# Scaling a weight matrix late: the first batch multiplies by lambda at its output

## The chip, the cores and the metric

The kernel runs on one core of one Trainium2 chip. The metric is device time in microseconds (us), as the median of several executions. Before the change it is 306.67 us, the median of 5 runs that lie between 305.12 and 307.16 us. TensorE, the matrix engine, is called PE below, and its weight loads are PEld. VectorE is DVE, ScalarE is ACT, GpSimd is POOL and SyncE is SP.

## The reference

Block-sparse attention over 4 batches, 8 heads, 768 tokens and head size 64 is followed by a residual MLP with affine scalings. Attention keeps a mask of blocks of 32: neighbours, first and last blocks, and three sampled blocks for each row of blocks. Then:

```python
a1 = alpha1 * x + beta1
tok = np.einsum('ts,bsd->btd', w_tok, a1)
u = x + lam * tok
a2 = alpha2 * u + beta2
ch = np.maximum(a2 @ w_ch1, 0.0) @ w_ch2
return (u + lam * ch).astype(np.float32)
```

`x` is the attention output, batch x 768 x 512. `w_ch1` is 512 x 2048 and `w_ch2` is 2048 x 512. `lam` has one value for each of the 512 output columns, so `lam * (h @ w_ch2)` equals `h @ (w_ch2 * lam)`: lambda may be multiplied into the columns of the weights, or into the result.

## The kernel before

**The tiling.** The 32 heads of the 4 batches are taken as 16 pairs of heads. The scores of one pair are cut into 9 units of 128 x 1024. For each unit PE multiplies queries and keys (L924 for the first six pairs, L943 for the other ten), ACT takes the exponential (L962), DVE multiplies by the mask (L967, only for pairs 6 to 15), and PE multiplies with the values (L986). DVE divides by the row sums (L1002, L1005). Then comes the token mixing, PE's L1207 with DVE's L1158, L1169, L1231 and L1245 around it.

**The channel MLP** works on half batches, counted `kk` from 0 to 7; `kk` 0 and 1 are batch 0. Its first product (L1354) makes 16 tiles of 128 x 384, each of four matmuls. ACT (L1393) or DVE (L1401) adds a bias, takes the relu and writes it to `hts`, of which there are two buffers. The second product (L1434) makes three output tiles (`mt`) of 128 x 512, each from four groups (`r`) of four matmuls, group `r` reading rows `4r` to `4r+3` of the weight tile `w2b`. DVE adds the result to `x_sb` (L1456), and SP sends it out (L1475). Half batch `kk` can start its first product only when `hts` has a free buffer, that is, when the second product of `kk - 2` is through.

**The second weights** are loaded by POOL in four DMAs (L588) and then scaled in place by DVE: eight instructions (L678) multiply two rows of blocks each by a bf16 copy of lambda (`lam_bcb`, L670). Every group of the second product depends on the two of them that scaled its rows (L1447).

**The start.** The first pair of heads does not go through POOL. SP and ACT issue its loads at L360 to L366: `sampi` and both heads of k on ACT's queue, both heads of q and then three small constant loads (`ind_dr`, L366) on SP's queue. Each head is cast to bf16 (L421), transposed by PE (L426) and copied out of PSUM by four DVE copies (L455), two for q and two for k, after which the first score matmul can run.

**The order of the work** is written by a planner (`Plan`, L104 to L271). Every operation has dependencies, a cost on each engine that may take it, and a due time. The planner walks through time and gives each free engine the ready operation with the earliest due time. Each engine then executes exactly that order (`pin_order`, L56). The engines start the plan at fixed times (L465: PE, ACT at 6200 ns, DVE at 6250 ns), and the loads of the second head of the first pair are assumed to land at the times in L894. Before the planner runs, the due times are shifted by random numbers from a list of seeds (L489 to L494). A new list, or another way of drawing, gives another order of everything on every engine.

Of the kernel before, what the change touches and what calls it, by code (L numbers as in the profile page):

```python
# [3 lines left out]

# [16 lines left out]
ALU = mybir.AluOpType  # L21
# [4 lines left out]
D = 64  # L26
# [3 lines left out]
DM = 512  # L30
FF = 4 * DM
P = 128
NT = S // P
# [10 lines left out]
NXB = 3  # L44
# [1 line left out]
EXPB = -0.35667494  # L46
T0 = 6
FINE = 3
SEEDS = [3000002, 3000003, 3000005, 3000006, 3000008, 3000027, 3000041, 3000052, 3000078, 3000097, 3000108, 3000114, 3000122, 3000127, 3000136, 3000180, 3000188, 3000206, 3000215, 3000219, 3000250, 3000263, 3000275, 3000280, 3000283, 3000293, 3000304, 3000326, 3000332, 3000343, 3000367, 3000440, 3000558, 3000615, 3000616, 3000621, 3000657, 3000851, 3000855, 3000993, 3001011, 3001012, 3001029, 3001046, 3001124, 3001231, 3001486, 3001568, 3001676, 3001731, 3001993, 3002553, 3003152, 3003308, 3003443, 3004176, 3005076, 3005643, 3006518, 3007963, 3008413, 3008734, 3008895]
NFILL = 24  # L50
ORD = ((0, 2, 4, 1, 3, 5), (1, 3, 5, 0, 2, 4))
HF = 3 * S
# [24 lines left out]
def dve(n, rate=1):  # L77
    return n / 0.96 / rate + 155
# [196 lines left out]
def kernel(  # L275
# [17 lines left out]
    nc = tc.nc  # L293
# [5 lines left out]
    ind_dr = nc.inline_tensor(ind_np, name="ind_c")  # L299
# [14 lines left out]
    kx2 = [t[:, 1, :, :] for t in qk2]  # L314
    qkr = [t[0:D].rearrange("p w h (g r t) -> p w h g r t", g=3, r=2) for t in qk2]
# [4 lines left out]
    x_sb = pp.tile([P, NXB * NT, DM], FP, name="x_sb", tag="x_sb")  # L320
    lam_bc = pp.tile([P, DM], FP, name="lam_bc", tag="lam_bc")
# [4 lines left out]
    lam_bcb = pp.tile([P, DM], BF, name="lam_bcb", tag="lam_bcb")  # L326
# [20 lines left out]
    ot = many(2, [P, DM], FP, "ot")  # L347
    rcp = many(2, [P, NT], FP, "rcp")
    MB = slice(D, KC)
# [4 lines left out]
    def pair_ap(src, b, n):  # L354
        return src[b, 2 * n : 2 * n + 2].rearrange("h (p o) d -> p h (o d)", o=NT)
# [4 lines left out]
    nc.scalar.dma_start(sampi[MB, :], sampled_blocks.bitcast(I32))  # L360
    nc.sync.dma_start(q2f[:, 0, :], pair_ap(q, 0, 0)[:, 0, :])
    nc.scalar.dma_start(k2f[:, 0, :], pair_ap(k, 0, 0)[:, 0, :])
    nc.scalar.dma_start(k2f[:, 1, :], pair_ap(k, 0, 0)[:, 1, :])
    nc.sync.dma_start(q2f[:, 1, :], pair_ap(q, 0, 0)[:, 1, :])
    for i in range(1, 4):
        nc.sync.dma_start(kx2[i // 2][MB, i % 2, :], ind_dr.ap())  # L366

# [29 lines left out]
    def where(out, what, op, lim):  # L399
# [9 lines left out]
        out=eqt[MB, :, 0:NR],  # L409
        in0=sampi[MB, 0 : 2 * NR : 2].unsqueeze(1).broadcast_to([NBLK, NBLK, NR]),  # L410
        in1=kbi[MB, :].unsqueeze(2).broadcast_to([NBLK, NBLK, NR]),
        op=ALU.is_equal,
    )
    nc.vector.tensor_reduce(
        out=mbb[MB, :], in_=eqt[MB], axis=mybir.AxisListType.X, op=ALU.max
# [14 lines left out]
    for w in (0, 1):  # L430
# [13 lines left out]
        out=qx2[0][MB, 0, 0:HS],  # L444
        in0=bq_ps[0][0:NBLK, 0:HS],
# [6 lines left out]
    for w in range(2):  # L452
        t = transposes(gbT[w][:], lambda o: relp[:, 0, w, ts(o, P)], range(3))
        for r in range(2):
            nc.vector.tensor_copy(  # L455
                out=qkr[0][:, w, 0, :, r, :], in_=t[r * D : (r + 1) * D, 0:3]
            )
    keep_warm(10, P)
    for t in vext:
        nc.vector.memset(t[:, :, :, D:VW], 1.0)  # L460
# [1 line left out]

    pl = Plan(
        dict(sps=2, gb=4, eT=NE, q=4, k=4, v=4, vx=3, qk=2, hts=2, a1p=2, ub=2, ot=2),
        dict(PE=6200, ACT=6200, DVE=6250, POOL=4000, SP=4000),  # L465
    )
    GB = [("gb", 0), ("sps", 0)]
    GL = [("gb", 0), ("sps", 0)]
# [1 line left out]
    def bank(key):  # L470
        p, j = pl.slot[key]
        return (gbT if p == "gb" else spsT)[j]

    def sl(key):
        return pl.slot[key][1]
# [64 lines left out]
    def landed(name, t):  # L540
        op = Op(name, [], 0, None)
        op.start, op.vis = 0, t
        return op
# [20 lines left out]
    W1, W2, BC = [], [], {}  # L564
    w2h = {}
# [66 lines left out]
    for g in range(4):  # L632
# [6 lines left out]
                deps=[x.tr for x in WTT],  # L639
# [9 lines left out]
        deps=[BC["a1"], BC["lam"]],  # L649
# [6 lines left out]
        deps=[BC["b1"], BC["lam"]],  # L656
# [6 lines left out]
        deps=[landed(("be2",), 6500)],  # L663
    )
    B1T = []
    LB = pl.dve(
        ("lamb",),
        dve(512, 2),
        46,
        lambda op: nc.vector.tensor_copy(out=lam_bcb[:], in_=lam_bc[:]),  # L670
        deps=[BC["lam"]],
    )
    W2S = []
    for g in range(8):

        def e_w2(op, g=g):
            w = w2h["t"][:, 2 * g : 2 * g + 2, :]
            nc.vector.tensor_tensor(  # L678
                out=w, in0=w, in1=lam_bcb[:].unsqueeze(1).broadcast_to([P, 2, DM]), op=ALU.mult
            )  # L680

        W2S.append(pl.dve(("w2s", g), dve(1024, 2), 52 + g, e_w2, deps=[W2[g // 2], LB]))


    last = None
# [202 lines left out]
    for i in range(2):  # L888
        op = pl.dve(
            ("fc", i),  # L890
            dve(384, 2),
            1 + 0.1 * i,
            lambda op, i=i: first_cast(1, i, nc.vector.tensor_copy),
            deps=[landed(("f", i), 5000 + 1350 * i)],  # L894
        )
        FC1.append(op)
    ROWS = []
# [10 lines left out]
    NORM = {}  # L908
    OT = {}
    CH1S = {}  # L910
    UTD = {}

    def unit_heads(u):
# [100 lines left out]
    for pi in range(NP):  # L1014
        b, n = divmod(pi, NPAIR)
# [7 lines left out]
        def e_v(op, pi=pi):  # L1023
# [10 lines left out]
            deps=[LD[("v", pi)]],  # L1034
# [6 lines left out]
    i = 0  # L1041
    while i < NI:
# [5 lines left out]
        deps = []  # L1048
# [14 lines left out]
        if pi == 0:  # L1063
            deps = [] if u < 4 else deps + ROWS[:1]
        if pi == 1:
            deps = deps + ROWS[1 : 2 if u < 4 else 3]
        occ = 437 if pi < T0 else 850
        op = pl.pe(
            ("qk", i),
            occ,  # L1070
            i - 0.7,
            e_qk,
            deps=deps,
            after=prevq[-1:],
            need=[(key, [("sps" if len(ks) == 1 else "gb", 0)]) for ks in keys for key in ks],
            uses=uses,
# [3 lines left out]
        for j, key in zip(batch, keys):  # L1080
# [6 lines left out]
                deps=[op],  # L1087
# [6 lines left out]
            if units[j][0] >= T0:  # L1094
# [5 lines left out]
                    deps=[ex] + MASK,  # L1100
# [3 lines left out]
            for a in unit_heads(uj):  # L1104
# [8 lines left out]
                    lambda op, part, pj=pj, uj=uj, a=a: emit_pv(op, part, pj, uj, a),  # L1113
# [10 lines left out]
    for pi in range(NP):  # L1124
# [211 lines left out]
        for hf in range(2):  # L1336
# [89 lines left out]
            for mt, c0, c1 in cuts:  # L1426
                t = 3 * hf + mt
                cs = slice(c0, c1)
                ck = ("cp", kk, mt, c0)
                for r in range(4):  # L1430

                    def e_c2(op, hk=hk, ck=ck, mt=mt, r=r, cs=cs):
                        for nk in range(4 * r, 4 * r + 4):
                            nc.tensor.matmul(  # L1434
                                bank(ck)[:, cs],
                                htsT[hk][:, nk, ts(mt, P)],
                                w2h["t"][:, nk, cs],
                                start=(nk == 0),
                                stop=(nk == 15),
                            )  # L1440

                    c2 = pl.pe(
                        ("ch2", kk, mt, r),
                        pe(4, 4 * (c1 - c0)),
                        d0 + 18 + (4 * mt + r) * 18 / 12 + c0 / 100,
                        e_c2,
                        deps=rel[4 * r : 4 * r + 4] + W2S[2 * r : 2 * r + 2],  # L1447
                        after=pc[-1:],
                        need=[(ck, GL)] if r == 0 else [],
                        uses=[hk] + ([] if r == 0 else [ck]),  # L1450
                    )
                    pc.append(c2)
                okey = ("ot", kk, mt, c0)

                def e_ot(op, okey=okey, ck=ck, b=b, t=t, cs=cs):
                    nc.vector.tensor_tensor(  # L1456
                        out=ot[sl(okey)][:, cs],
                        in0=x_sb[:, b % NXB * NT + t, cs],
                        in1=bank(ck)[:, cs],
                        op=ALU.add,  # L1460
                    )

                o = pl.dve(
                    ("ot", kk, mt),
                    dve(c1 - c0),
                    d0 + 18 + 18 / 12 * 4 * mt - 2,
                    e_ot,
                    deps=[c2],
                    need=[(okey, [("ot", 0)])],
                    uses=[ck],  # L1470
                )
                OT[(b, t)] = o

                def e_out(op, okey=okey, b=b, t=t, cs=cs):
                    nc.sync.dma_start(  # L1475
                        out[b].rearrange("(p o) d -> p o d", o=NT)[:, t, cs],
                        ot[sl(okey)][:, cs],
                    )

                pl.add(  # L1480
                    ("out", kk, mt),
                    [("SP", 450, beside(350, 450, 90))],
                    0,
                    e_out,
                    deps=[o],
                    uses=[okey],
                )

    for seed in SEEDS:
        r = random.Random(seed)  # L1490
        part, step = r.choice([0.01, 0.03, 0.1, 0.3]), r.choice([0.5, 1.5, 4])
        for op, due in zip(pl.ops, [op.due for op in pl.ops]):
            if r.random() < part and op.due0 < 300:
                op.due = due + r.gauss(0, step)
    pl.run()
    pin_order(nc, tc)

# [29 lines left out]
```

## Time and profile before

| | |
|---|---|
| median of 5 runs | 306.67 us |
| the profiled execution, its own time | 307.16 us |
| its span, first to last instruction | 305.4 us |
| granted PE clock | 1.000 |
| PE busy | 299.7 us |
| DVE busy | 229.0 us |
| ACT busy | 179.8 us |
| POOL busy | 44.8 us |

The profile comes from one execution. Its own time is 0.49 us above the median of the runs, and 1.76 us of it lie outside the span. PE's busy time counts overlapping matmuls once, but it also counts the time that a matmul needs to fill and drain. A PE that is 98% busy is therefore not proof that it streams data 98% of the time. A matmul of 512 columns is shown with some 380 ns, yet a run of them starts one every 216 ns. Where it matters the text works with these distances from start to start.

### The profile page before, as it was taken

The numbers are of one execution on the slowest core, as the hardware profiler recorded it, in microseconds if no ns is written. First come the engines' busy times: TensorE is split into PE (matmuls) and PEld (weight loads), VectorE is DVE, ScalarE is ACT, GpSimd is POOL, SyncE is SP. The second block draws the span as 40 slices with busy tenths as digits, with TensorE's granted clock in tenths as the row PEclk, the third lists the DMA queues.
The fourth block names the chain that finished last, engine by engine and source line by source line (L and its number), as shares of the span: only waits on it lengthen the run. The fifth ranks groups of instructions, "written<-read, shape, count | busy, mean of one in ns | idle before, by whom it ended". The sixth has DMA issues, their size and how long they took to land.

```text
span 305.4 us, 7168 instructions
## 1 busy us (share of the span) xinstructions
PE 299.7 (98%) x2970; PEld 188.4 (62%) x2996; DVE 229.0 (75%) x434; ACT 179.8 (59%) x246; POOL 44.8 (15%) x71
## 2 busy tenths in 40 slices
PE   8998999999999999999999999999999999999997
PEld 4776877766655575556654675555755574555545
DVE  7669999998888786978685797867986863837622
ACT  3998889897697847887467835768756410000000
POOL 9365344323002000120000000000000000000000
PEclk9999999999999999999999999999999999999999
DMA  7999999999669628763160406132002004000012
GB/s 161 194 240 199 206 203 206 200 154 178 108 119 114 137 28 146 144 115 63 55 146 13 102 36 120 46 80 68 2 24 64 34 8 136 16 34 34 36 65 73
DMA packets 50672, 31.38 MB, mean 103 GB/s; under 512 B 27784, under 2 KB 47056, under 8 KB 50640
## 3 DMA queue, kind: packets, MB, share of 16 engines
q0 software_dynamic: 17520, 15.47, 34.3%
q1 hardware_dynamic: 32796, 15.06, 21.2%
q8 instruction: 23, 0.38, 0.5%
q10 hardware_dynamic: 324, 0.39, 0.4%
q14 instruction: 9, 0.07, 0.1%
HBM read 30.78 MB, written 6.29 MB: 121 GB/s over the span
## 4 chain that ended last, share of the span: by engine, by line
PE 87%; DMA 7%; POOL 2%; ACT 2%; issue 1%; DVE 1%; POOLq 0%; ACTq 0%
PE gb L1434 27%; PE gb L1354 27%; PE gb L1207 10%; PE gb L986 10%; PE sps L943 4%; PE sps L924 4%; DMA wtk<-in_moe_w_tok_dram 3%; DMA q<-in_q_dram 3%; PE gb L943 3%; ACT eT L962 2%; PE gb L426 1%; DVE eT L967 1%; POOL k L552 0%; POOL wtokT L379 0%; POOL wtk L574 0%
## 5 line engine op out<-in xcount | busy, mean ns | idle before, releaser
L962 ACT ACTIVATE eT<-sps 128x1024 f16<-128x1024 f32 x114 | 111.0, 1032 | 8.2 <-PE sps L924 7.3
L1354 PE MATMUL gb<-uT,w1b 128*128 128x384 bf16 (+1 forms) x512 | 93.7, 326 | 0.0
L1434 PE MATMUL gb<-w2b,hts 128*128 128x512 bf16 (+2 forms) x374 | 88.5, 370 | 1.4 <-issue 0.2
L1354 PEld LDWEIGHTS <-w1b 128*128 128x128 bf16 x512 | 47.7, 98 | 33.7 <-issue 3.2
L967 DVE TENSOR_TENSOR eT<-eT,msk 128x1024 f16<-128x1024 f16 x90 | 59.3, 685 | 5.4 <-ACT eT L962 5.4
L986 PEld LDWEIGHTS <-eT 128*128 128x128 f16 x1152 | 48.6, 97 | 18.1 <-issue 3.4
L1434 PEld LDWEIGHTS <-hts 128*128 128x128 bf16 x400 | 36.4, 98 | 37.0 <-issue 1.9
L986 PE MATMUL gb<-vext,eT 128*128 128x65 f16 x1152 | 54.0, 193 | 0.5 <-ACT eT L962 0.2
L1393 ACT ACTIVATE hts<-gb,b1t 128x384 bf16<-128x384 f32 x64 | 36.8, 584 | 27.3 <-PE gb L1354 24.2
L962 ACT ACTIVATE eT<-gb 128x512 f16<-128x512 f32 x60 | 32.5, 595 | 32.7 <-PE gb L943 32.6
L1401 DVE TENSOR_SCALAR hts<-gb,b1t 128x384 bf16<-128x384 f32 x64 | 39.3, 616 | 15.4 <-PE gb L1354 14.4
L1456 DVE TENSOR_TENSOR ot<-x_sb,gb 128x512 f32<-128x512 f32 (+2 forms) x25 | 16.6, 664 | 26.4 <-PE gb L1434 26.3
L1207 PE MATMUL gb<-a1p,wtokT 128*128 128x256 bf16 (+1 forms) x360 | 34.6, 251 | 0.0
L924 PE MATMUL sps<-qk 88*128 88x512 bf16 (+1 forms) x144 | 32.8, 333 | 0.6 <-ACT eT L962 0.2
L1207 PEld LDWEIGHTS <-wtokT 128*128 128x128 bf16 x360 | 29.2, 98 | 4.0
L1231 DVE TENSOR_TENSOR x_sb<-x_sb,gb 128x512 f32<-128x512 f32 (+1 forms) x26 | 16.7, 645 | 6.9 <-PE gb L1207 6.7
L1005 DVE TENSOR_TENSOR x_sb<-gb,rcp 128x384 f32<-128x384 f32 x32 | 17.8, 557 | 1.1
L943 PE MATMUL sps<-qk 64*128 64x256 bf16 x180 | 17.9, 305 | 0.0
L943 PEld LDWEIGHTS <-qk 64*128 64x128 bf16 x240 | 9.2, 94 | 11.5 <-issue 6.6
L552 POOL DMA_DIRECT2D q<-in_q_dram x15 | 10.7, 711 | 38.0 <-DMA qk<-q 33.6
L1245 DVE TENSOR_TENSOR ub<-x_sb,a_bc 128x512 bf16<-128x512 f32 (+1 forms) x26 | 15.9, 644 | 0.1
L1158 DVE TENSOR_TENSOR a1p<-x_sb,a_bc 128x768 bf16<-128x768 f32 (+1 forms) x17 | 15.4, 906 | 0.2
(67 smaller groups left out, 163.7 us busy)
## 6 DMA issues: line engine op xcount, KB each, us to landing
out_dram<-ot SPq DMA_DIRECT2D x23, 256.0 KB, 2.2
v<-in_v_dram POOLq DMA_DIRECT2D x16, 192.0 KB, 9.6
k<-in_k_dram POOLq DMA_DIRECT2D x15, 192.0 KB, 8.4
q<-in_q_dram POOLq DMA_DIRECT2D x15, 192.0 KB, 9.5
w1b<-in_moe_w_ch_dram POOLq DMA_DIRECT2D x4, 512.0 KB, 12.4
w2b<-in_moe_w_ch_dram POOLq DMA_DIRECT2D x4, 512.0 KB, 11.5
qk<-qk SPq DMA_DIRECT2D x20, 96.0 KB, 2.9
wtk<-in_moe_w_tok_dram POOLq DMA_DIRECT2D x3, 384.0 KB, 9.2
```

Of the source, the lines that this page charges most:

```text
L924: nc.tensor.matmul(spsT[sl(key[0])][:, o : o + w], kx2[i][0:KC, a, ts(jt, P)], qx2[i][0:KC, a, c : c + w], start=True, stop=True,)
L943: nc.tensor.matmul(half(key, r)[:, o : o + w], kd[i][rows, h, g, :], qx2[i][rows, h, c : c + w], start=True, stop=True,)
L962: nc.scalar.activation(out_, in_, AF.Exp, bias=EXPB, scale=SCALE)
L967: nc.vector.tensor_tensor(out=e, in0=e, in1=msk[:, :, x : x + 512], op=ALU.mult)
L986: nc.tensor.matmul(bk[:, t * VW : t * VW + D + 1], eTt[sl(("eT", i))][:, ts(col, P)], vx[:, a, jt, 0 : D + 1], start=(r == 0), stop=(r >= ...
L1005: nc.vector.tensor_tensor(out=x_sb[:, s0 : s0 + NT, h * D : (h + 1) * D], in0=o[:, :, 0:D], in1=rc[:].unsqueeze(2).broadcast_to([P, NT, D] ...
L1207: nc.tensor.matmul(bank(bk)[:, j * wp * P : (j + 1) * wp * P], wtokT[:, s, ts(m * g + j, P)], a1p[sl(ak)][:, s, 0:wp, :].rearrange("p w c ...
L1231: nc.vector.tensor_tensor(out=s, in0=s, in1=tp, op=ALU.add)
L1354: nc.tensor.matmul(bank(bk)[:, 0 : HS + w0], w1b[:, dk, ts(f, P)], rhs[dk], start=(dk == 0), stop=(dk == 3),)
L1393: nc.scalar.activation(htsT[hk][:, f, :], bank(bk)[:, w0 : HS + w0], AF.Relu, bias=b1t[:, f : f + 1], scale=1.0,)
L1401: nc.vector.tensor_scalar(out=htsT[hk][:, f, :], in0=bank(bk)[:, w0 : HS + w0], scalar1=b1t[:, f : f + 1], scalar2=0.0, op0=ALU.add, op1=A ...
L1434: nc.tensor.matmul(bank(ck)[:, cs], htsT[hk][:, nk, ts(mt, P)], w2h["t"][:, nk, cs], start=(nk == 0), stop=(nk == 15),)
```

## The change

Four things are edited.

1. **Second weights.** The eight scaling instructions are no longer issued when the weights have landed. The first batch (`kk` 0 and 1) multiplies by unscaled weights, and its second product depends on the load of its rows only. Its output takes two DVE instructions in place of one: PSUM times `lam_bc` into `ot`, then `x_sb` plus `ot` into `ot`. The scaling instructions are added to the plan behind the second product of `kk` 1, with due times 96 to 99.5 in place of 52 to 59. The two for the rows of group `r` depend on all six products of the first batch that read these rows; from `kk` 2 on, group `r` depends on the two of them, as before.
2. **The start.** The three constant loads on SP's queue are issued between the two heads of q, and no longer behind them. The two copies of k out of PSUM move from DVE to ACT.
3. **The planner's constants.** The engines' start times and the assumed landing times of the second head change.
4. **The random shifts.** The list of seeds is another, and each seed now shifts only operations whose due time is near a random middle.

```diff
     nc.scalar.dma_start(k2f[:, 0, :], pair_ap(k, 0, 0)[:, 0, :])
+    for i in range(1, 4):
+        nc.sync.dma_start(kx2[i // 2][MB, i % 2, :], ind_dr.ap())
     nc.scalar.dma_start(k2f[:, 1, :], pair_ap(k, 0, 0)[:, 1, :])
     nc.sync.dma_start(q2f[:, 1, :], pair_ap(q, 0, 0)[:, 1, :])
-    for i in range(1, 4):
-        nc.sync.dma_start(kx2[i // 2][MB, i % 2, :], ind_dr.ap())
...
         for r in range(2):
-            nc.vector.tensor_copy(
-                out=qkr[0][:, w, 0, :, r, :], in_=t[r * D : (r + 1) * D, 0:3]
-            )
+            cp = nc.scalar.copy if w else nc.vector.tensor_copy
+            cp(out=qkr[0][:, w, 0, :, r, :], in_=t[r * D : (r + 1) * D, 0:3])
...
-        dict(PE=6200, ACT=6200, DVE=6250, POOL=4000, SP=4000),
+        dict(PE=5800, ACT=6050, DVE=5800, POOL=4000, SP=4000),
...
     W2S = []
-    for g in range(8):
-
-        def e_w2(op, g=g):
-            w = w2h["t"][:, 2 * g : 2 * g + 2, :]
-            nc.vector.tensor_tensor(
-                out=w, in0=w, in1=lam_bcb[:].unsqueeze(1).broadcast_to([P, 2, DM]), op=ALU.mult
-            )
-
-        W2S.append(pl.dve(("w2s", g), dve(1024, 2), 52 + g, e_w2, deps=[W2[g // 2], LB]))
+
+    def scale_w2(readers):
+        for g in range(8):
+
+            def e_w2(op, g=g):
+                w = w2h["t"][:, 2 * g : 2 * g + 2, :]
+                lam2 = lam_bcb[:].unsqueeze(1).broadcast_to([P, 2, DM])
+                nc.vector.tensor_tensor(out=w, in0=w, in1=lam2, op=ALU.mult)
+
+            W2S.append(
+                pl.dve(
+                    ("w2s", g),
+                    dve(1024, 2),
+                    96 + g / 2,
+                    e_w2,
+                    deps=readers[g // 2] + [LB],
+                )
+            )
...
-            deps=[landed(("f", i), 5000 + 1350 * i)],
+            deps=[landed(("f", i), 5600 - 500 * i)],
...
-                        deps=rel[4 * r : 4 * r + 4] + W2S[2 * r : 2 * r + 2],
+                        deps=rel[4 * r : 4 * r + 4] + (W2S[2 * r : 2 * r + 2] if kk > 1 else [W2[r]]),
...
+                    if kk < 2:
+                        RD.setdefault(r, []).append(c2)
...
-                    nc.vector.tensor_tensor(
-                        out=ot[sl(okey)][:, cs],
-                        in0=x_sb[:, b % NXB * NT + t, cs],
-                        in1=bank(ck)[:, cs],
-                        op=ALU.add,
-                    )
+                    o = ot[sl(okey)][:, cs]
+                    x = x_sb[:, b % NXB * NT + t, cs]
+                    ps_ = bank(ck)[:, cs]
+                    if b == 0:
+                        nc.vector.tensor_tensor(out=o, in0=ps_, in1=lam_bc[:, cs], op=ALU.mult)
+                        nc.vector.tensor_tensor(out=o, in0=x, in1=o, op=ALU.add)
+                    else:
+                        nc.vector.tensor_tensor(out=o, in0=x, in1=ps_, op=ALU.add)
...
-                    dve(c1 - c0),
+                    dve(c1 - c0) * (2 if b == 0 else 1),
...
+                if kk == 1 and mt == 2:
+                    scale_w2(RD)
...
-        part, step = r.choice([0.01, 0.03, 0.1, 0.3]), r.choice([0.5, 1.5, 4])
-        for op, due in zip(pl.ops, [op.due for op in pl.ops]):
-            if r.random() < part and op.due0 < 300:
-                op.due = due + r.gauss(0, step)
+        part, step = r.choice([0.02, 0.1, 0.3, 1]), r.choice([0.3, 1, 3])
+        mid, wide = r.uniform(0, 300), r.choice([4, 12, 40])
+        for op in pl.ops:
+            if abs(op.due0 - mid) < wide and r.random() < part:
+                op.due += r.gauss(0, step)
```

The two lists of seeds (63 numbers before, 52 after) are left out.

More of the change, by code (lines that the diff above doesn't have):

```diff
@@ L1 @@
-import random
 import random
@@ L48 @@
 FINE = 3
-SEEDS = [3000002, 3000003, 3000005, 3000006, 3000008, 3000027, 3000041, 3000052, 3000078, 3000097, 3000108, 3000114, 3000122, 3000127, 3000136, 3000180, 3000188, 3000206, 3000215, 3000219, 3000250, 3000263, 3000275, 3000280, 3000283, 3000293, 3000304, 3000326, 3000332, 3000343, 3000367, 3000440, 3000558, 3000615, 3000616, 3000621, 3000657, 3000851, 3000855, 3000993, 3001011, 3001012, 3001029, 3001046, 3001124, 3001231, 3001486, 3001568, 3001676, 3001731, 3001993, 3002553, 3003152, 3003308, 3003443, 3004176, 3005076, 3005643, 3006518, 3007963, 3008413, 3008734, 3008895]
+SEEDS = [2368360002, 2368360005, 2368360008, 2368360022, 2368360028, 2368360031, 2368360050, 2368360067, 2368360083, 2368360085, 2368360089, 2368360096, 2368360144, 2368360155, 2368360159, 2368360198, 2368360204, 2368360219, 2368360231, 2368360262, 2368360291, 2368360306, 2368360309, 2368360457, 2368360521, 2368360740, 2368360741, 2368360761, 2368360886, 2368360958, 2368361005, 2368361131, 2368361149, 2368361207, 2368361276, 2368361304, 2368361308, 2368361391, 2368361405, 2368361424, 2368361614, 1368351946, 1368351960, 1368352029, 1368352547, 1368352791, 1368352820, 2368362950, 2368362973, 2368363005, 2368363029, 1368353383]
 NFILL = 24
@@ L910 @@
     CH1S = {}
+    RD = {}
     UTD = {}
```

## The prediction

> **What bounds the kernel now.** First the page's shares and slices, to see which engine is full and where.
>
> ```profile
> PE 299.7 (98%) x2970; PEld 188.4 (62%) x2996; DVE 229.0 (75%) x434; ACT 179.8 (59%) x246; POOL 44.8 (15%) x71
> ...
> DVE  7669999998888786978685797867986863837622
> ACT  3998889897697847887467835768756410000000
> ```
>
> DVE is nearly full only in slices 4 to 10 (23 to 76 us); ACT is full up to about 70 us and has nothing left behind 245 us. PE is busy everywhere, so the question is how much of that is streaming. I took the start times of all matmuls in the trace and counted as lost whatever a distance from start to start exceeds the steady distance of its shape (0.216 us for 512 columns, 0.163 for 384, 0.109 for 256, 0.055 for 128, 0.030 for the value products). From 9 us to the end this gives 13.4 us lost: 0.72 in 10 to 20, 1.96 in 20 to 30, 0.08 in 30 to 40, 0.93 in 40 to 50, 0.54 in 50 to 60 (4.2 us in all) and 9.2 us behind 60, spread at 0.2 to 0.9 for each 10 us. The last is the drain around each L943 batch and each change of product; the change leaves these alone. So **PE is the bound**, and what an edit away from PE can win lies mostly ahead of 60 us. The waits and the timeline show the largest piece there:
>
> ```profile
> 26.72 0.40 PE L986 MATMUL gb<-vext,eT 128*128 128x65 f16 x8
> ...
> 27.86 0.34 PE L426 MATMUL gb<-identb,q 128*128 128x128 bf16 x3 [0.74 <-DMA q<-in_q_dram]
> ```
>
> PE stands 0.9 us here (26.93, the last value product, to 27.86) for a load of q. The chain of waits has this load too ("DMA wtk" from 6.25, then "DMA q" 18.09 to 27.8): ahead of 28 us the chain is POOL's queue of loads, and its first issues are not touched by the edit.
>
> Then the instructions that the change touches, by group and in time:
>
> ```profile
> L678 DVE TENSOR_TENSOR w2b<-w2b,lam_bcb 128x1024 bf16<-128x1024 bf16 x8 | 5.4, 681 | 0.0
> L648 DVE TENSOR_TENSOR a_bc<-a_bc,lam_bc 128x512 f32<-128x512 f32 x1 | 0.7, 678 | 0.0
> L1456 DVE TENSOR_TENSOR ot<-x_sb,gb 128x512 f32<-128x512 f32 x23 | 15.8, 685 | 24.2 <-PE gb L1434 24.1
> ```
>
> The eight scalings (51.3 to 69.5 us) are far ahead of their first use at 81.5 us.
>
> **Part 1, the start.** Rows:
>
> ```profile
> 1.20 0.41 SPq L364 DMA_DIRECT2D q2f<-in_q_dram  x1
> 1.40 0.36 ACTq L362 DMA_DIRECT2D k2f<-in_k_dram  x1
> 1.67 1.20 SPq L366 DMA_DIRECT2D qk<-ind_c  x3
> ...
> 4.29 0.51 ACT L421 CAST relp<-k2f 128x384 bf16<-128x384 f32 x1 [0.74 <-DMA k2f<-in_k_dram]
> 4.83 0.48 ACT L440 ACTIVATE qk<-gb 24x384 bf16<-24x384 f32 x1
> 4.92 1.50 DVE L455 COPY qk<-gb 64x384 bf16<-64x384 bf16 x4 [0.42 <-PE gb L426]
> ```
>
> ACT waits 0.74 us for the first head of k. In front of it on the wire are both heads of q. The second moves behind three issues of 0.40 us, from 1.20 to 2.40, and the three small loads (36 KB each, 108 KB) go ahead of it in place of its 192 KB. The 84 KB difference is 0.5 us at the 161 GB/s of the first slice; k lands earlier by 0 to 0.5, I take 0.3. The copies: DVE's four end at 6.42, and the first k copy, which the first score matmul needs, at about 6.05. On ACT the k copies come behind L440 (ends 5.31) at some 0.48 each (L440's row, the nearest PSUM source of 384 columns): 5.9 and 6.3. That is 0.1 better; with k earlier 0.4, so the first score matmul moves from 6.22 to about 5.8. The price: the second head of q lands 1.2 us later, by the median of 2.5 us at 4.9; its cast is at 7.65, so nothing. Everything up to 26.9 us could come 0.4 earlier (ACT is 9.9 of 10 us busy in 10 to 20). Then PE meets the load of q at 27.86, which hangs on POOL's queue, and waits longer. Between 0 and -0.4; nearest to the former, **-0.1**.
>
> **Part 2, scaling leaves 51 to 69 us.** DVE instructions without a wait between them start faster than their duration: three L967 of 0.685 take 1.89, one each 0.60 us. So eight of L678 take 8 x 0.605 = 4.84 us of DVE. DVE was 9.39 and 9.70 us busy in 50 to 60 and 60 to 70, PE lost 0.54 and 0.10 there. The gain is between 0 and 0.64, because PE can't win back more than it lost; the 0.93 of 40 to 50 lies ahead of the first scaling. DVE is the fullest engine there, so near the upper end: **-0.5**. The first product of batch 0 fills PE from 56 us on, so DVE's relief beyond that is earlier work, not time.
>
> Here a rule of the Trainium skill differs from the row: "VectorE: DVE Perf Modes", section "The DRAIN you can't avoid", says that a next instruction starts only when the pipeline has emptied (and points to a later section for exceptions). By it the scalings hold DVE for 8 x 0.681 = 5.45 us. The row decides: 4.84. The sum stays as it is, since PE's 0.64 caps the gain in both.
>
> **Part 3, two output instructions in the first batch.** Six outputs at 86.6 to 148.4 us. L1456's 0.685 for the PSUM product (same shape), then an addition in SBUF, row L648, 0.678, which reads what was just written. A dependent pair is L1158 and L1169: starts 104.92 and 105.92, 1.00 apart at a duration of 0.96, so 0.04 more. Added: 6 x 0.72 = 4.3 us of DVE in 62 us, where it idles 10 to 35% of each 10 us. "VectorE: DVE Perf Modes", "Rules for kernel authors", speaks against this: chained instructions gain nothing by being close, one should keep their number low. By the rule alone, all exposed, the sum is +4.3; by the row it is hidden in idle time of DVE, and the output DMA behind it has no reader. The bank comes free after the first of the two as before, though the planner reckons it with the second. From 0 to +4.3; **0**.
>
> **Part 4, scaling in place between batches 0 and 1.** In the trace the last second product of `kk` 1 ends at about 148.4 and the first of `kk` 2 is at 151.7.
>
> ```profile
> 144.00:149.00 5.00, 4.95 (x54) 3.32 (x53) 3.24 (x6) 0.30 (x2) 0.00 (x0) 1.00 0.00 0
> 149.00:154.00 5.00, 4.95 (x56) 3.52 (x56) 3.83 (x7) 3.81 (x6) 0.00 (x0) 1.00 0.36 97
> 154.00:159.00 5.00, 5.00 (x39) 2.49 (x37) 4.03 (x9) 3.26 (x5) 0.00 (x0) 1.00 0.72 144
> 159.00:164.00 5.00, 4.95 (x32) 2.45 (x32) 4.02 (x7) 4.26 (x7) 0.00 (x0) 1.00 0.32 86
> ```
>
> The columns are the stretch, its length, and the busy time of PE, PEld, DVE, ACT and POOL. DVE has 1.76 + 1.17 + 0.97 + 0.98 = 4.9 us idle in these 20; the scalings need 4.84. The rows of groups 0 to 2 come free before 148, and relus can go to ACT (8.4 us idle). If a scaling waits for PE, mask multiplications (L967), relus (L1401) and normalisations stand behind it on DVE, and value products and second products wait for those. PE's cover is the first product of `kk` 3, 16 groups of 0.65 = 10.4 us, free as soon as `kk` 1 has released `hts`, and attention. Between 0 and +4.84; with cover twice the need, **+0.2**. No DMA and no other queue is moved past.
>
> **Part 5, the order drawn anew.** No row shows it. At best it removes the rest of what is lost ahead of 60 us: 4.2 - 0.6 = -3.6; at worst it loses as much, +3.6. What can be redrawn is the 1.96 of 20 to 30 and the 0.93 of 40 to 50, together 2.9: an earlier place for that q load in POOL's queue takes 0.9 of it, and DVE with 4.84 us less to do in 51 to 69 leaves room to take up what was late. I take less than half, **-1.2**. This is the least certain term.
>
> **Sum:** -0.1 - 0.5 + 0 + 0.2 - 1.2 = -1.6. The profiled execution's 307.16 becomes 305.56; it stands 0.49 above the median, so the median is **305.1 us**, 0.5% less.
>
> **Rivals.**
> *Nothing reaches the end:* PE is the bound, its work is the same, the start gets stuck at the load of q, and DVE's relief falls into time that PE filled anyway. For it: PE lost 0.10 in 60 to 70 although DVE was 9.70 busy. Against it: 4.2 us of loss ahead of 60. Terms 1, 2 and 5 are near nothing: 306.67 + 0.2 - 0.2 = 306.6 us.
> *The order removes nearly all loss ahead of 60:* -3.6 and -0.5 with +0.2: 306.67 - 3.9 = 302.8 us.
> *Slower, PE stands before batch 1:* the first `kk` 2 groups are queued on PE behind scalings that DVE hasn't reached. Two scalings take 1.21 us, the four matmuls that they free 0.86, so a PE with nothing else in its queue would stand up to 4.84 us; 60% of it, 2.9, ends at 309.6. It decides once PE has fewer than 4.84 / 0.65 = 8 first-product groups of `kk` 3 ahead of them, or DVE's backlog is longer than the 4.9 us idle. The trace has DVE and ACT with little to spare there once 4.3 us of part 3 are added; against it is that the plan knows the dependency.
>
> **How the numbers follow.** About 0.5% (1.5 us) is what a measurement of this kernel can tell from no change: faster is below 305.1, slower above 308.2. The forecast has a chance of 0.44, its own range 303.8 to 306.3, and 0.28 of it is faster and 0.16 the same. Nothing reaches the end: 0.24, of it 0.03 faster, 0.20 the same, 0.01 slower. Nearly all loss removed: 0.12, faster. Slower: 0.20, of it 0.01 the same. So faster 0.43, same 0.37, slower 0.20. The range leaves out one in ten on each side: below, the better half of the 302.8 case, at 302.8; above, half of the slower case, at 308.8.
>
> **What would show it.** Right: the first score matmul near 5.8; no L678 ahead of 100 us; twelve output instructions of about 0.68 in batch 0; L678 at 140 to 160 beside PE's first products; PE's last matmul near 301. Step 1 is wrong if the first score matmul stays at 6.2, or the gain is still there behind the load of q. Step 2 is wrong if PE loses as much in 50 to 70 as before. Step 4 is wrong if PE idles behind DVE L678. The prediction fails if PE's loss ahead of 60 us stays at 4 us, or the loss behind it, 9.2, moves by more than 1.

## The result and the profile after

The changed kernel takes 307.63 us (median of 43 runs) against 306.65 us (80 runs). The ratio is 1.0039, 95% interval 1.0029 to 1.0049: slower by 1.0 us in the medians, where 1.6 us less was forecast. The ratio is not the quotient of the two medians (here 1.0032). Below, too, the two can differ, by up to 0.16%; the interval belongs to the ratio.

The profiled execution has 307.06 us (span 305.3), 0.57 below its own median, while that of before is 0.49 above its own. Side by side the two profiles therefore look equal, and only stages can be compared, not their ends. The page after, engines and slices, and the groups that the change made:

```profile
PE 298.6 (98%) x2968; PEld 187.1 (61%) x2996; DVE 238.5 (78%) x446; ACT 176.2 (58%) x240; POOL 44.8 (15%) x71
...
DVE  6579898788999797979997697969986683885712
ACT  5899899874587847776557657747777000000000
...
L679 DVE TENSOR_TENSOR w2b<-w2b,lam_bcb 128x1024 bf16<-128x1024 bf16 x8 | 5.4, 684 | 0.0
L1471 DVE TENSOR_TENSOR ot<-x_sb,ot 128x512 f32<-128x512 f32 x6 | 4.2, 692 | 0.2
L1470 DVE TENSOR_TENSOR ot<-gb,lam_bc 128x512 f32<-128x512 f32 x6 | 4.1, 687 | 0.8 <-PE gb L1442 0.8
```

The change does what it says: eight scalings of 0.684 us, now at 141.7 to 153.9 us, and twelve output instructions in the first batch. DVE has 9.5 us more to do: 4.2 for the second output instruction and 8.1 for relus, of which the new order gave it 77 instead of 64 (47.4 us instead of 39.3); it has some 2.8 us less of other work. The busy digits of DVE move from the stretch ahead of 76 us to 80 and 150 us.

What PE lost, by the prediction's way of counting (distance from start to start beyond the steady one of the shape, from 9 us on; where a distance is just two steady ones, a record is missing and nothing is counted), in us:

| kernel | 9 to 60 | 60 to 100 | 100 to 200 | behind 200 | sum |
|---|---|---|---|---|---|
| before | 4.2 | 1.7 | 4.9 | 2.6 | 13.4 |
| after | 3.1 | 2.6 | 5.6 | 2.8 | 14.1 |

Two things limit this table. The profiles of before and after lack 26 and 28 of 2996 matmuls (PE x2970 and x2968 against PEld x2996 on the pages), and where the lost one has another shape than its neighbour, this way of counting takes it for a loss. And each line is one execution. The experiments below put both right.

Ahead of 60 us the table shows a gain. The load of q that PE stood for is in time now (timeline, PE):

```profile
26.54 0.41 PE L994 MATMUL gb<-vext,eT 128*128 128x65 f16 x8
26.78 0.33 PE L425 MATMUL gb<-identb,q 128*128 128x128 bf16 x3
```

But that is not the new order's doing. The kernel `e1_before_newstart`, described below, has the order of before on every engine, and its profile shows no stand at this place either:

```profile
26.80 0.41 PE L985 MATMUL gb<-vext,eT 128*128 128x65 f16 x8
27.17 0.34 PE L426 MATMUL gb<-identb,q 128*128 128x128 bf16 x3
```

Nor do the profiles of e3 and e7, which have that order and the old start as well. The 0.9 us belong to the one profiled execution of before, in which this load landed late.

Behind 60 us the changed kernel loses more. Busy time by stretch, of before and then of after (columns: stretch, length, PE, PEld, DVE, ACT, POOL, granted clock, DMA share, GB/s):

```profile
80.00:100.00 20.00, 19.78 (x203) 11.61 (x203) 15.93 (x28) 15.52 (x25) 2.11 (x3) 1.00 0.68 99
...
140.00:160.00 20.00, 19.84 (x182) 12.17 (x185) 15.16 (x27) 12.17 (x19) 0.00 (x0) 1.00 0.32 72
```

```profile
80.00:100.00 20.00, 19.37 (x225) 12.25 (x227) 18.89 (x34) 15.62 (x24) 2.11 (x3) 1.00 0.67 110
...
140.00:160.00 20.00, 19.89 (x197) 12.63 (x196) 19.89 (x36) 11.90 (x18) 0.00 (x0) 1.00 0.24 60
```

DVE is full at 140 to 160, where it scales, without PE suffering; at 80 to 100, with 3 us more of DVE, PE loses most. That looks as if DVE's added work were the culprit. The experiments say otherwise.

### The profile page after: what moved, and what is told of

The parts are those of the page before. It is cut to its first block, busy times and chain, and to the rows that moved or that the text cites. A ratio compares the mean times of both kernels' runs of the same rounds, so it can differ in the third digit from the quotient of the medians.

```text
span 305.3 us, 7165 instructions
## 1 busy us (share of the span) xinstructions
PE 298.6 (98%) x2968; PEld 187.1 (61%) x2996; DVE 238.5 (78%) x446; ACT 176.2 (58%) x240; POOL 44.8 (15%) x71
## 4 chain that ended last, share of the span: by engine, by line
PE 86%; ACT 6%; DVE 4%; issue 2%; DMA 1%; SPq 0%; ACTq 0%
PE gb L1442 27%; PE gb L1362 25%; PE gb L994 10%; PE gb L1215 10%; ACT eT L970 5%; PE sps L932 5%; PE sps L951 4%; PE gb L951 3%; DMA q2f<-in_q_dram 1%; PE sps L1362 1%; PE gb L425 1%; DVE eT L975 1%; DVE ot L1471 0%; DVE ot L1470 0%; ACT qk L479 0%
## 5 line engine op out<-in xcount | busy, mean ns | idle before, releaser
L1362 PE MATMUL gb<-uT,w1b 128*128 128x384 bf16 (+1 forms) x492 | 90.8, 326 | 0.4 <-DVE x_sb L1013 0.3
L994 PEld LDWEIGHTS <-eT 128*128 128x128 f16 x1152 | 49.3, 97 | 20.5 <-issue 5.1
L994 PE MATMUL gb<-vext,eT 128*128 128x65 f16 x1152 | 55.0, 193 | 1.5 <-DVE vext L1032 1.2
L1409 DVE TENSOR_SCALAR hts<-gb,b1t 128x384 bf16<-128x384 f32 x72 | 44.3, 616 | 10.5 <-PE gb L1362 8.9
L1401 ACT ACTIVATE hts<-gb,b1t 128x384 bf16<-128x384 f32 x51 | 29.5, 583 | 33.3 <-PE gb L1362 32.4
L932 PE MATMUL sps<-qk 88*128 88x512 bf16 (+1 forms) x144 | 31.8, 325 | 0.7 <-ACT eT L970 0.4
L1473 DVE TENSOR_TENSOR ot<-x_sb,gb 128x512 f32<-128x512 f32 (+2 forms) x19 | 12.5, 659 | 18.4 <-PE gb L1442 18.3
L1010 DVE RECIPROCAL rcp<-gb 128x6 f32<-128x6 f32 x32 | 6.2, 193 | 16.2 <-PE gb L994 15.9
L1013 DVE TENSOR_TENSOR x_sb<-gb,rcp 128x384 f32<-128x384 f32 x32 | 17.8, 557 | 1.1
L550 POOL DMA_DIRECT2D q<-in_q_dram x15 | 10.6, 708 | 38.8 <-DMA qk<-q 31.6
```

The source lines that it names most:

```text
L932: nc.tensor.matmul(spsT[sl(key[0])][:, o : o + w], kx2[i][0:KC, a, ts(jt, P)], qx2[i][0:KC, a, c : c + w], start=True, stop=True,)
L994: nc.tensor.matmul(bk[:, t * VW : t * VW + D + 1], eTt[sl(("eT", i))][:, ts(col, P)], vx[:, a, jt, 0 : D + 1], start=(r == 0), stop=(r >= ...
L1013: nc.vector.tensor_tensor(out=x_sb[:, s0 : s0 + NT, h * D : (h + 1) * D], in0=o[:, :, 0:D], in1=rc[:].unsqueeze(2).broadcast_to([P, NT, D] ...
L1362: nc.tensor.matmul(bank(bk)[:, 0 : HS + w0], w1b[:, dk, ts(f, P)], rhs[dk], start=(dk == 0), stop=(dk == 3),)
L1401: nc.scalar.activation(htsT[hk][:, f, :], bank(bk)[:, w0 : HS + w0], AF.Relu, bias=b1t[:, f : f + 1], scale=1.0,)
L1409: nc.vector.tensor_scalar(out=htsT[hk][:, f, :], in0=bank(bk)[:, w0 : HS + w0], scalar1=b1t[:, f : f + 1], scalar2=0.0, op0=ALU.add, op1=A ...
```

## The experiments

Three theories. **A:** the order that the new list of seeds gives is worse; the edits themselves cost nothing. **B:** the weights' part costs, through the doubled output (B1) or the late scalings (B2). **C:** the new start costs.

### Taking the start apart

The start stands ahead of the planner, so it can be exchanged with every planned order kept.

**e1_before_newstart**, the kernel before with the start's two edits:

```diff
+    for i in range(1, 4):
+        nc.sync.dma_start(kx2[i // 2][MB, i % 2, :], ind_dr.ap())
     nc.scalar.dma_start(k2f[:, 1, :], pair_ap(k, 0, 0)[:, 1, :])
...
-            nc.vector.tensor_copy(
+            cp = nc.scalar.copy if w else nc.vector.tensor_copy
```

> The kernel before with the two edits of the start alone (the three constant loads between the heads of q, the two copies of k on ACT); the planned order, its constants and its seeds are those of before, so every engine executes the planned work in the same order. Theory A (the redrawn order is what made it slower): the start wins 0 to 0.4 us, 306.3 to 306.7. Theory B (late scaling and the doubled output made it slower): the same, 306.3 to 306.7. Theory C (the new start itself costs, through a later second head of q or ACT's queue): 307.3 to 307.7.

Measured: 306.13 us against 306.65, ratio 0.9990 (0.9973 to 1.0006).

**e2_after_oldstart**, the changed kernel with these two edits undone:

> The changed kernel with the old start (constant loads last, all four copies on DVE); its planned order is kept, with its constants. Theories A and B: the start's gain is lost in part, 307.6 to 308.0. Theory C: 306.7, back to the kernel before.

Measured: 307.91 us, ratio 1.0040 (1.0026 to 1.0054); the changed kernel was 307.63, ratio 1.0039. Neither shows a cost of the new start, so C falls. Whether it wins is not clear of noise: 0.10% by e1's ratio, whose interval reaches no change, and 0.01% by the ratios of e2 and the changed kernel (0.28 us by their medians). With the old start on both sides the weights and the order together cost 0.40%, 1.2 us (e2 against before); with the new one 1.0039 / 0.9990, 0.49%, 1.5 us.

The profiles of e1 and e2 have all 2996 matmuls, and so they show better than the table above where the two orders lose. By the same count (it comes out within 0.2 us of the table's lines), in us:

| kernel | 9 to 60 | 60 to 100 | 100 to 200 | behind 200 | sum |
|---|---|---|---|---|---|
| e1, order of before | 3.2 | 1.8 | 3.8 | 1.8 | 10.6 |
| e2, order of after | 3.3 | 2.5 | 4.2 | 1.8 | 11.9 |

The order of after loses as much ahead of 60 us and 1.1 us more behind it, most of that at 60 to 100.

### Moving the weights' part between the two orders

**e3_before_latescale** keeps the order of before on every engine and moves only the scalings:

```diff
-        W2S.append(pl.dve(("w2s", g), dve(1024, 2), 52 + g, e_w2, deps=[W2[g // 2], LB]))
+        W2S.append(
+            pl.dve(("w2s", g), dve(1024, 2), 52 + g, lambda op: None, deps=[W2[g // 2], LB])
+        )
+        W2E.append(e_w2)
...
+                    if e == "DVE":
+                        self.late(None, t, False)
```

`late` emits one scaling behind each planned DVE instruction from where the last second product of the first batch is through; the first batch's output is doubled as in the change.

> The order of before on every engine, but the eight scalings are taken out of 51 to 69 us and put, one behind each DVE instruction, from where the plan has the last second product of the first batch done (about 146 us), and the first batch's output takes two DVE instructions. Seeds, start and constants as before. Theory A: the mechanism is hidden, 306.4 to 306.9. Theory B: 307.3 to 308.0, with PE waiting for DVE at 80 to 110 us or at 148 to 156 us. Theory C: 306.7.

Measured: 310.33 us, ratio 1.0118 (1.0095 to 1.0140). It is much worse than any theory had it: 3.7 us. The timeline shows how DVE's added work gets to PE:

```profile
152.05 0.68 DVE L696 TENSOR_TENSOR w2b<-w2b,lam_bcb 128x1024 bf16<-128x1024 bf16 x1
...
152.65 0.68 DVE L1483 TENSOR_TENSOR ot<-gb,lam_bc 128x512 f32<-128x512 f32 x1
...
153.38 1.47 PE L1228 MATMUL gb<-a1p,wtokT 128*128 128x256 bf16 x12 [0.67 <-DVE ot L1483]
```

The output (L1483) stands behind a scaling in DVE's queue. It holds the PSUM bank that PE's next matmul is to write, so PE stands 0.67 us.

**e4_after_earlyscale** is the opposite: the order of after, the scalings emitted at the plan times that they have in the kernel before, one output instruction.

```diff
+        if g < 8 and t >= when[g] and W2[g // 2].vis and W2[g // 2].vis <= t and LB.vis:
...
-                    e_w2,
+                    lambda op: None,
...
-                    if b == 0:
+                    if False:
```

> The order of the changed kernel on every engine, but the eight scalings are put at the plan times that they have in the kernel before (49 to 67 us) and the first batch's output is one DVE instruction again. Seeds, start and constants as after. Theory A: 307.4 to 307.9, as slow as the changed kernel. Theory B: 306.4 to 306.9. Theory C: 307.6.

Measured: 309.59 us, ratio 1.0092 (1.0073 to 1.0110): 2.0 us slower than the changed kernel. The stretch from 60 to 70 us, in the changed kernel and then here:

```profile
60.00:70.00 10.00, 10.00 (x109) 6.66 (x108) 8.79 (x27) 7.63 (x10) 3.52 (x5) 1.00 1.38 172
```

```profile
60.00:70.00 10.00, 8.65 (x87) 5.46 (x86) 9.93 (x29) 6.84 (x9) 3.03 (x5) 1.00 1.12 157
```

With the scalings DVE is full and PE loses. Both crossings are slower than both kernels, against every theory, so neither tells what the mechanism costs. Work put into an order that doesn't know it was expensive at both places.

### Taking the weights' part out of the changed kernel

The same order again, but work is taken away, so that nothing comes as a surprise to it. These kernels leave a part of the computation out, as the expectations say.

**e5_after_oneop**: in the first batch's output, `if b == 0:` becomes `if False:`.

> The changed kernel with one output instruction in the first batch in place of two (x plus the product): lambda is left out of the first batch's output, so that part of the computation is missing. The order of all else is kept. Theory A (the order itself is worse): 307.3 to 307.7. Theory B1 (the six added DVE instructions hold PE's banks at 80 to 150 us): 306.6 to 306.9, with the loss at 80 to 100 us gone.

**e6_after_noscale**: the planned scalings emit nothing (`e_w2` becomes `lambda op: None`).

> The changed kernel without the eight late scalings: batches 1 to 3 multiply by unscaled weights, so lambda is left out there. The order of all else is kept. Theory A: 307.3 to 307.7. Theory B2 (the late scalings stop PE at 142 to 154 us): 306.6 to 307.0.

**e56_after_neither**: both.

> Both taken out: no scaling at all and one output instruction; lambda is left out of the second product everywhere. The order of all else is kept. Theory A: 307.2 to 307.6, no faster than e5 and e6. Theories B1 and B2: the sum of what e5 and e6 give, down to 306.0.

Measured, against 306.41 for the kernel before:

| run | us | ratio | interval |
|---|---|---|---|
| e5, one output instruction | 307.40 | 1.0041 | 1.0018 to 1.0064 |
| e6, no scaling | 307.85 | 1.0062 | 1.0037 to 1.0086 |
| e56, neither | 307.48 | 1.0044 | 1.0024 to 1.0063 |

With up to 9.6 us less of DVE (4.2 + 5.4 by the groups above) the time stays where it was. PE's loss in e56 is 3.1, 2.6, 5.3 and 2.8 in the table's four stages, close to the changed kernel's. The timeline shows why. First after, then e56, at the same place in the order:

```profile
98.46 0.19 DVE L1010 RECIPROCAL rcp<-gb 128x6 f32<-128x6 f32 x1
98.68 0.56 DVE L1013 TENSOR_TENSOR x_sb<-gb,rcp 128x384 f32<-128x384 f32 x1
...
99.30 1.46 PE L1362 MATMUL gb<-uT,w1b 128*128 128x384 bf16 x8 [0.28 <-DVE x_sb L1013]
```

```profile
99.23 0.20 DVE L1010 RECIPROCAL rcp<-gb 128x6 f32<-128x6 f32 x1 [0.65 <-PE gb L994]
99.46 0.56 DVE L1013 TENSOR_TENSOR x_sb<-gb,rcp 128x384 f32<-128x384 f32 x1
...
100.07 1.46 PE L1362 MATMUL gb<-uT,w1b 128*128 128x384 bf16 x8 [0.50 <-DVE x_sb L1013]
```

The value products (L994) of a pair end, DVE normalises (L1010, L1013) and so frees the bank, and PE's next first-product group needs just that bank. In e56 DVE has been waiting for PE for 0.65 us when it starts, and PE stands all the same. This stand is a round trip from PE over DVE to PE with nothing placed in between; it belongs to the order, not to DVE's load. So the added work does not cost in the changed kernel's order as it stands, and B falls in this form. Whether late scaling leads to a worse order is another question, asked further below.

### What an added instruction costs in an order that doesn't know it

**e7_before_doubled**: the kernel before with one more dependent DVE instruction at each of six outputs.

```diff
+                    if b == 0:
+                        o = ot[sl(okey)][:, cs]
+                        nc.vector.tensor_tensor(out=o, in0=o, in1=o, op=ALU.max)
```

> The kernel before with one more DVE instruction behind each of the first batch's six outputs (the maximum of ot with itself, same shape and types as the added one, dependent on the instruction ahead); scalings stay early, nothing else moves. Theory A: hidden, 306.5 to 306.9. Theory B1: 307.3 or more; the earlier run with scalings moved as well was at 310.3, and this run says how much of its 3.7 us belongs to the doubled output.

Measured: 308.78 us against 306.41, ratio 1.0088 (1.0063 to 1.0112): 2.4 us for six instructions of 0.69, or 4.2 us of DVE. By the count above PE loses 1.5 us more at 100 to 200 us than in the profile of before (6.4 against 4.9, with 26 matmuls missing in both). Busy time at 100 to 120 us, and PE's wait there:

```profile
100.00:120.00 20.00, 19.04 (x195) 12.08 (x195) 17.10 (x29) 13.07 (x19) 2.11 (x3) 1.00 0.52 95
```

```profile
100.79 0.69 DVE L1464 TENSOR_TENSOR ot<-ot 128x512 f32<-128x512 f32 x1
101.40 1.28 DVE L967 TENSOR_TENSOR eT<-eT,msk 128x1024 f16<-128x1024 f16 x2
...
102.14 0.42 PE L986 MATMUL gb<-vext,eT 128*128 128x65 f16 x8 [0.43 <-DVE eT L967]
```

DVE is 17.10 of 20 us busy, so 2.9 us are idle in this stretch, and PE still waits: the mask multiplication (L967) stands behind the added instruction (L1464), later than the order was made for, and the value products that need it are next in PE's fixed order. Theory A had this hidden and missed.

### Other draws of the order

If the order is the cause, another list of seeds must move the time, with the weights' part late or early. The early kernel is the changed one, new start and constants included, with the scaling and the output planned as before:

```diff
-                    96 + g / 2,
+                    52 + g,
...
-                    deps=readers[g // 2] + [LB],
+                    deps=[W2[g // 2], LB],
...
-                    dve(c1 - c0) * (2 if b == 0 else 1),
+                    dve(c1 - c0),
```

For each, two lists of seeds came from the same search: seeds tried in turn from unshifted due times, each kept when the planner's own end came earlier, 6000 trials.

> The changed kernel (late scaling, doubled output, new start and constants) with another list of seeds: 6000 trials from unshifted due times, kept when the planner's own end came earlier; first of two draws. Theory A (what was measured is the draw of the order, not the mechanism): the draws of late and of early scatter over each other, all within 306 to 309. Theory B (late scaling leaves the planner less room, at 80 to 150 us, where its outputs hold banks longer): both late draws behind both early draws by 1 us or more; this one at 307.8 to 309.

> The same as s1_late, second draw with other random numbers. Theory A: within the scatter of the other three. Theory B: 307.4 to 308.5, behind both early draws.

> The changed kernel with its new start and constants, but the scaling planned early again (due 52 to 59, before any second product) and one output instruction: the weights' part of the change undone inside the planner. Seeds from the same search, 6000 trials from unshifted due times; first of two draws. Theory A: 306 to 309, scattered among the late draws. Theory B: 306.0 to 306.7, ahead of both late draws by 1 us or more.

> The same as s1_early, second draw. Theory A: within the scatter of the other three. Theory B: 305.8 to 306.6.

Then the search was carried on, for the late kernel from the changed kernel's own list, for the early one from its second draw, and, as the other end, the list was left empty.

> The changed kernel with its own seeds and more of them behind: the same search carried on for 20000 further trials. Nothing else differs. Theory A (the order's draw is the cause, late scaling is free once the plan knows it): 304.8 to 306.2, ahead of the changed kernel by 1.5 us or more and ahead of the kernel before. Theory B (late scaling costs): not ahead of the kernel before, 306.5 to 307.5.

> The second early draw (new start, early scaling, one output instruction) with its search carried on for 15000 trials. Theory A: 305.2 to 306.6, within 0.5 us of d_late. Theory B: 305.2 to 306.2, ahead of d_late by 1 us or more.

> The changed kernel with an empty list of seeds, so no due time is shifted. Both theories: slower by far, 315 to 322, because the first order is unfinished. Theory A: within 2 us of n_early, either way. Theory B: behind n_early by 1 us or more.

> Early scaling and one output instruction with the new start, empty list of seeds. 315 to 322; theory A: within 2 us of n_late, theory B: ahead of it.

Measured (the kernel before: 306.49 with the four s runs, 306.42 with the others):

| order | late scaling: us, ratio, interval | early scaling: us, ratio, interval |
|---|---|---|
| empty list (n) | 314.37, 1.0256, 1.0225 to 1.0287 | 314.16, 1.0250, 1.0220 to 1.0281 |
| 6000 trials, first draw (s1) | 307.57, 1.0051, 1.0032 to 1.0071 | 306.48, 1.0008, 0.9991 to 1.0025 |
| 6000 trials, second draw (s2) | 306.82, 1.0025, 1.0009 to 1.0042 | 306.75, 1.0012, 0.9997 to 1.0027 |
| searched on (d) | 305.69, 0.9986, 0.9968 to 1.0003 | 306.05, 0.9987, 0.9970 to 1.0003 |

The list of seeds alone moves the late kernel from 314.37 to 305.69, 8.7 us (the empty lists came out just below the 315 that was expected).

Without any search late and early differ by 0.06%, and searched on by 0.01%, far inside the intervals; the two long searches were not equal, though, in length or start. In between, with 6000 trials on both sides, late is behind early: by 0.43% in the first pair, whose intervals don't meet, and by 0.13% in the second, whose intervals do. Theory A had these four scatter over each other, and they don't. Theory B had 1 us or more between each late and each early draw, and only the first pair has it (1.1 us).

The changed kernel's list, with its ratio of 1.0039, lies between the two late draws, so it is an ordinary one. The two late draws stand at 1.0038 on average and the two early ones at 1.0010. By these four runs alone, up to 0.28 of the 0.39% could come from late scaling making a good order harder to find. Two draws each can't settle this.

`d_late` keeps every edit of the change and its list of seeds, with more seeds behind, and is 0.9986 / 1.0039 = 0.9947 of the changed kernel. Against the kernel before it is lower in its median by 0.7 us, but the interval reaches 1.0003. Its busy time by stretch:

```profile
80.00:100.00 20.00, 19.89 (x232) 12.81 (x233) 18.45 (x34) 15.79 (x24) 2.12 (x3) 1.00 0.75 115
...
140.00:160.00 20.00, 19.89 (x199) 12.81 (x198) 18.78 (x33) 13.76 (x22) 0.00 (x0) 1.00 0.17 33
```

DVE is as full at 80 to 100 us as in the changed kernel (18.45 against 18.89), and PE, with 19.89 in place of 19.37, doesn't stand there as it did. PE's loss is 2.4, 1.5, 5.1 and 2.6: against the changed kernel 0.7, 1.1, 0.5 and 0.2 less. So late scaling as such doesn't force the changed kernel's time: with the same edits a better order takes it away.

## Why the prediction was wrong

**What bounds the kernel** held: PE. But of the 4.2 us of loss ahead of 60 us, the 0.9 for the load of q was an accident of the one profiled execution; e1, with the same order, loses 3.2 there. And some of the 9.2 us behind 60 are matmuls without a record.

**Part 1, the start, -0.1 (0 to -0.4):** inside its range, but not told from nothing: -0.3 by e1's ratio, with an interval from -0.8 to +0.2. That the first score matmul is at 5.60 in the profile after, forecast near 5.8, is luck: over the fourteen profiles with the new start it lies between 5.60 and 7.13. The sum had a slip, too: 5.31 + 0.48 is 5.8, not 5.9. The start's lead was lost before the load of q: the first exponential ends at 7.45 us in the profile after, against 8.34, but the tenth at 17.41, against 17.51. In between, the profile after has a stand for the copy of the first v that the one of before hasn't:

```profile
9.31 0.40 PE L994 MATMUL gb<-vext,eT 128*128 128x65 f16 x8 [1.16 <-DVE vext L1032]
```

**Part 2, scaling leaves 51 to 69 us, -0.5:** not shown as a gain. PE's loss in 50 to 70 went from 0.64 to 0.51, but by the same count e2, with the order of after, has as much as before again. That DVE has no room there is shown by e4, in the changed kernel's order; the kernel before had an order in which the same work was covered. The row that decided against the rule holds in the changed kernel: there too the instruction behind a scaling starts 0.60 us after it.

**Part 3, doubled output, 0:** right for this kernel (e5), wrong as it was argued. I read 10 to 35% idle time of DVE as cover. e7 has such idle time and loses 2.4 us of the 4.3 that the prediction had as its worst case. What e5 and e7 together suggest is that an added instruction is covered when the order behind it was drawn with its duration, so that PE has other work ahead of what the instruction delays.

**Part 4, scaling between the batches, +0.2:** right; e6 wins nothing by leaving it out.

**Part 5, the order drawn anew, -1.2:** the step that failed, in sign. With the same start on both sides, the new order and the weights' part cost 1.2 to 1.5 us, and taking the weights' part out of that order wins nothing back (e5, e6, e56). Two readings of the profile misled the term. It counted 2.9 us of loss at 20 to 30 and 40 to 50 us as what can be redrawn, and 0.9 of that, the load of q, was met by one execution of the old order and not by e1, e3 and e7. By the complete profiles nothing was won ahead of 60 us: 3.2 in e1, 3.3 in e2. And it left out the loss behind 60 us, which I had called drain and said "the change leaves these alone". A new order redraws it as well: from e1 to e2 it rose by 1.1 us, 0.7 of that at 60 to 100 (1.8 us from before to after in the first table). That was the prediction's own sign of failure. A redraw also has no reason to go down. Of the seven searched lists measured here, five have a ratio above 1 to the kernel before. The term should have been centred above nothing.

**The rivals:** the slower one named the wrong mechanism. PE didn't stand before batch 1: in the profile after it is busy for 19.89 of the 20 us from 140, and e6, without the late scalings, is no faster. The rival by which nothing reaches the end (306.6) came nearest, but it had no term for a worse order either.

What stays open: whether late scaling makes a good order harder to find (the s runs lean that way, the n and d runs don't), and so how much of the order's cost is chance; and which single placement in the changed order costs how much. The planner's new constants were not tried apart from the seeds; every kernel of the s, n and d runs has them. One stand of 0.28 to 0.50 us is shown above, no more.

## What to carry to other kernels

Where a program's whole order is drawn by a search, an edit that changes costs or dependencies also throws the order away, and the new draw can outweigh the edit: here 8.7 us of spread over lists of seeds, against 0.01 to 0.43% (0.03 to 1.3 us) between late and early in the four pairs. Compare such edits with the same search behind both sides and with several draws of each, or with the order pinned and work only taken out; work put into a pinned order measures the surprise (2.4 us for six instructions whose like costs nothing measurable in an order drawn with them). Idle time of an engine is cover only if the engines that wait for it have something else in front in their own order. And before a wait is put down to an order, look for it in a second execution: the stand of 0.9 us for the load of q was in one of four executions of the old order.

## What the runs showed that was not expected

The first load of k lands at very different times in programs with the same start. ACT's cast of it starts at 4.04 us in the profile after and in `d_late`, at 5.12 in `s2_late`; over the fourteen profiles with the new start it lies between 4.04 and 5.21, over the four with the old one between 4.29 and 5.46. That is more than the 1.0 us under study, and a reason why one pair of profiles can't be compared by its ends.

The first five score matmuls also come in two speeds, at a granted clock that the profile gives as 1.00 in both cases. Before and after (timeline, PE):

```profile
6.22 1.91 PE L924 MATMUL sps<-qk 88*128 88x512 bf16 x5
```

```profile
5.60 1.22 PE L932 MATMUL sps<-qk 88*128 88x512 bf16 x5
```

The distance of two of 512 columns is 0.427 us in the former and 0.216 once PE runs fully. The Trainium skill, "TensorE: Matmul & The Clock Gate", has a cold distance of N / 1.2 GHz (0.427 us at 512 columns; Part 2, "Back-to-back issue gap") and, in Part 1, a window that runs free of the kernel's start, which fits that programs with the same start show either: with the new start, the profile after has 0.216 us, e1 has 0.427. The window itself is shown by no run here.
